# Memory peaks of batches 2 to 7 by VectorE and GpSimd instead of TensorE, with another plan of the order

## The chip, the cores and the metric

The kernel runs on one core of one Trainium2 chip. The metric is device time in microseconds (us) of one execution; runs of one kernel are compared by their medians. The engines are named as the profile names them: PE is TensorE (PEld its weight loads), DVE is VectorE, ACT is ScalarE, POOL is GpSimd, SP is SyncE, which issues nearly all DMAs.

## The reference, cut to what matters

Attention over 32 learned memories per head feeds a mixture of experts of which each token uses one. There are 8 batches, 8 heads, 576 tokens, 64 columns per head.

```python
a = phi - np.max(phi, axis=2, keepdims=True)        # softmax over the 576 tokens, for each memory
a = np.exp(a)
a = a / (np.sum(a, axis=2, keepdims=True) + 1e-09)
k_m = np.einsum('bhsm,bhsd->bhmd', a, k)            # 32 memory keys and values per head
v_m = np.einsum('bhsm,bhsd->bhmd', a, v)
scores = scale * np.matmul(q, k_m.transpose(0, 1, 3, 2))
attn = softmax(scores)                               # over the 32 memories
x = np.matmul(attn, v_m)                             # (tokens, 8 * 64), heads side by side
...
e_idx = np.argmax(x @ w_gate + modality_bias[modality_id], axis=1)
h = np.maximum(x[mask] @ w1[e], 0.0)                 # expert e of the token, 512 -> 1024 -> 512
out[mask] = gate_w[mask, None] * (h @ w2[e])
```

The change concerns the first line: the maximum of `phi` over the tokens, for each head and memory, and how it comes back to all rows before the subtraction.

## The kernel before, in words

**The work of one batch.** It has two halves that are woven together. The *attention* half: `mem_max` (maxima of `phi`), `mem_top`, `mem_exp` (subtract and exponential), `mem_sums`, `mem_kv` (memory keys and values), `mem_turn` (their transposes), `scores`, then the softmax in small steps (`soften`, `normalise`, `a_split`), `mem_gate`, `logits` and `gate`. The *expert* half: `value_weights` (memory values times the expert's first matrix, L645), `hidden` (L678: 8 column blocks of 6 matmuls for each of two parts of the tokens, then relu `hh` on ACT, L687, and rest `hl` on DVE, L690) and `outputs` (L707: tiles of 24 matmuls of 512 columns, then `ob` on ACT, L720, and the store). A float is carried as two halves, high and low, so each product takes three matmuls.

**The layout of `phi`.** One tile `ph` holds a batch: the 128 partitions are 2 groups of heads (g) by 64 rows of tokens, the free axis is 4 heads (j) by 9 tokens by 32 memories. `mem_max` folds the 9 tokens on DVE with four tensor_tensor (L259, L260, L262, L263; 512, 256, 128 and 128 columns) into `top`, 128 x (4 heads x 32 memories). What is left is a maximum over the 64 partitions of each group. Before, `mem_top` turns `top` on PE (L143) and reduces on DVE over the 64 columns of each group (L274, `topc`); `mem_exp` spreads the result again over 64 partitions with two PE matmuls against the identity (L288), and the subtraction (L294) reads it from PSUM. Then ACT takes the exponential (L297) and GpSimd folds the sums over tokens (`mem_sums`, L259 to L263 on POOL). `kv_products` has 72 small products (L328, of two passes each) and 8 for the sums (L336), which wait for GpSimd. `kv_divide` makes a reciprocal on DVE (L412, L414) and scaled copies `keys` and `values` on ACT (L424, L422); `mem_turn` turns them on PE (L143) and copies them out on ACT (`kT`, L454, `vT`, L462); `scores` (L504) needs `kT`.

**What sets the order.** Every engine works its instructions in the order in which the program issues them. `weave` issues the stages of the two halves: each half has a fixed list; the attention's stages have a due time in units of expert progress. `TAKES` gives each stage kind an estimated PE time and a chain of other engines' times ("D1.9" is 1.9 us of DVE, A is ACT, P is POOL), with which `weave` keeps a clock, the time when each engine is free, and when a stage may go. An expert stage that starts a product takes one of four PSUM banks in a ring (`ps_e`, `bufs=4`): block f + 4 of `hidden` may start once `hl` of block f is done. The experts' list has `value_weights` of the next batch within the third and the fourth tile of `outputs` (for batch 1: right behind the third and within the fourth); it needs `mem_turn` of that batch, and the experts go no further until it is issued.

## Time and profile before

| | |
|---|---|
| median of 3 runs | 402.3 us (402.03 to 402.81) |
| the profiled execution | 401.36 us |
| its span, first to last instruction | 399.6 us |
| granted TensorE clock | 0.993 |
| busy, share of the span | PE 96%, PEld 77%, DVE 60%, ACT 36%, POOL 10% |
| DMA | 56.91 MB, mean 142 GB/s |

How to read it: rows of the timeline and of the chain of work that ended last begin with the start in us from the span's start and the duration in us; a row's `xN` merges N instructions. Matmuls are pipelined, so a matmul's record is longer than its share of PE: what it costs is read from start to start. The group rows give `busy us, mean ns` behind the bar, then the idle time before the group.

### The profile page before, as it was taken

Reading aid. Unit: us, or ns where it says so; the run is one execution under the profiler, and the core shown is the slowest. Engines: PE = TensorE matmul, PEld = TensorE weight load, DVE = VectorE, ACT = ScalarE, POOL = GpSimd, SP = SyncE. Lnnn points to the kernel's source line nnn. Section 1 sums busy time; section 2 is a strip of 40 time slices with the busy share of each in tenths; the row PEclk is TensorE's granted clock in tenths of the full one; section 3 lists DMA queues with packets and bytes.
Section 4 is the critical chain, followed back from the end, with each engine's and each line's share of the span. In section 5 each row is a group of like instructions: output and inputs, shape, how many; then the busy total and the mean of one; then the engine's idle time right before and its main releaser. Section 6 shows DMA issues by size and latency. Waiting matters only on the chain.

```text
span 399.6 us, 10090 instructions
## 1 busy us (share of the span) xinstructions
PE 385.6 (96%) x4235; PEld 306.5 (77%) x4235; DVE 239.1 (60%) x588; ACT 143.6 (36%) x342; POOL 40.7 (10%) x87
## 2 busy tenths in 40 slices
PE   6889999999999999999999999999999999999993
PEld 2547885979779787787878878788867879687982
DVE  2687857875697366744686546863488437770400
ACT  1255333516243333432443323433442425340410
POOL 4158020002000200020000200002000200000000
PEclk9999999999999999999999999999999999999999
DMA  6999158525740671627411391614411011341112
GB/s 229 356 381 389 41 157 315 201 107 138 281 131 28 209 260 55 224 72 269 143 26 54 89 345 38 244 47 132 160 26 30 26 30 29 132 159 28 30 27 59
DMA packets 28967, 56.91 MB, mean 142 GB/s; under 512 B 3312, under 2 KB 8432, under 8 KB 28912
## 3 DMA queue, kind: packets, MB, share of 16 engines
q1 hardware_dynamic: 28624, 56.16, 42.1%
q8 instruction: 35, 0.57, 0.6%
q14 instruction: 20, 0.16, 0.1%
q10 hardware_dynamic: 288, 0.01, 0.0%
HBM read 37.29 MB, written 18.87 MB: 141 GB/s over the span
## 4 chain that ended last, share of the span: by engine, by line
PE 90%; DVE 5%; DMA 1%; ACT 1%; issue 1%; ACTq 0%
PE pe L707 52%; PE pe L678 23%; PE pair L328 4%; PE pe L645 4%; PE pair L504 3%; DMA ph<-in_phi_dram 1%; PE pair L592 1%; PE pair L143 1%; PE pair L162 1%; PE pair L288 1%; DVE vwl L658 1%; PE pair L353 1%; DVE hl L690 1%; DVE t2top L259 0%; DVE q_sb L492 0%
## 5 line engine op out<-in xcount | busy, mean ns | idle before, releaser
L707 PE MATMUL pe<-w2h,hh 128*128 128x512 f32 x288 | 117.9, 410 | 0.4 <-DVE hl L690 0.4
L707 PE MATMUL pe<-w2h,hl 128*128 128x512 f32 x288 | 112.4, 390 | 0.0
L707 PE MATMUL pe<-w2l,hh 128*128 128x512 f32 x288 | 110.5, 392 | 0.0
L690 DVE SCALAR_TENSOR_TENSOR hl<-pe,hh 128x256 fp32r<-128x256 f32 (+2 forms) x160 | 58.8, 394 | 50.9 <-ACT hh L687 50.2
L707 PEld LDWEIGHTS pe<-w2h,hh 128*128 128x128 f32 x288 | 54.0, 188 | 23.9 <-issue 11.5
L687 ACT ACTIVATE hh<-pe 128x256 fp32r<-128x256 f32 (+2 forms) x160 | 53.8, 362 | 37.9 <-PE pe L678 36.7
L707 PEld LDWEIGHTS pe<-w2l,hh 128*128 128x128 f32 x288 | 54.0, 188 | 12.1
L707 PEld LDWEIGHTS pe<-w2h,hl 128*128 128x128 f32 x288 | 54.2, 188 | 9.5
L720 ACT ACTIVATE ob<-pe,gates 128x512 f32<-128x512 f32 x36 | 24.7, 689 | 80.7 <-PE pe L707 39.9
L678 PE MATMUL pe<-xbh,vwh 128*128 128x320 f32 x128 | 39.7, 310 | 0.0
L678 PE MATMUL pe<-xbl,vwh 128*128 128x320 f32 x128 | 39.4, 308 | 0.0
L678 PE MATMUL pe<-xbh,vwl 128*128 128x320 f32 x128 | 39.4, 307 | 0.0
L678 PE MATMUL pe<-xah,vwh 128*128 128x256 f32 x128 | 36.0, 290 | 0.2 <-DVE hl L690 0.2
L259 POOL TENSOR_TENSOR t2sums<-exp 128x512 f32<-128x512 f32 x7 | 9.0, 1288 | 259.0 <-ACT exp L297 259.0
L678 PE MATMUL pe<-xal,vwh 128*128 128x256 f32 x128 | 35.1, 283 | 0.0
L678 PE MATMUL pe<-xah,vwl 128*128 128x256 f32 x128 | 35.0, 282 | 0.0
L531 DVE STREAM_TRANSPOSE a<-pair 128x256 f32<-128x256 f32 (+1 forms) x32 | 13.6, 461 | 24.3 <-PE pair L504 24.3
L678 PEld LDWEIGHTS pe<-xah,vwh 128*128 128x128 f32 x128 | 23.9, 191 | 1.9 <-DVE hl L690 1.0
L678 PEld LDWEIGHTS pe<-xbh,vwh 128*128 128x128 f32 x128 | 24.0, 187 | 0.6 <-issue 0.3
L678 PEld LDWEIGHTS pe<-xal,vwh 128*128 128x128 f32 x128 | 24.0, 191 | 0.3
L678 PEld LDWEIGHTS pe<-xbl,vwh 128*128 128x128 f32 x128 | 24.0, 188 | 0.3
L678 PEld LDWEIGHTS pe<-xbh,vwl 128*128 128x128 f32 x128 | 24.0, 188 | 0.0
(135 smaller groups left out, 436.1 us busy)
## 6 DMA issues: line engine op xcount, KB each, us to landing
kv_sb<-in_k_dram SPq DMA_DIRECT2D x8, 1152.0 KB, 5.5
kv_sb<-in_v_dram SPq DMA_DIRECT2D x8, 1152.0 KB, 9.5
out_dram<-ob SPq DMA_DIRECT2D x64, 128.0 KB, 2.4
q_sb<-in_q_dram SPq DMA_DIRECT2D x7, 1152.0 KB, 6.8
ph<-in_phi_dram SPq DMA_DIRECT2D x8, 576.0 KB, 4.2
raw<-in_moe_w_dram SPq DMA_DIRECT2D x2, 1024.0 KB, 9.8
raw<-in_moe_w_dram SPq DMA_DIRECT2D x1, 1280.0 KB, 11.3
out_dram<-ob SPq DMA_DIRECT2D x4, 256.0 KB, 2.1
```

The source lines that it names most:

```text
L143: nc.tensor.transpose(dst, src, ident[:rows, :rows])
L162: nc.tensor.matmul(idle, lhsT=busy[:, 0:P], rhs=busy, start=True, stop=True)
L259: eng.tensor_tensor(t2, src[:, :, 0:4 * M], src[:, :, 4 * M:8 * M], op=op)
L328: nc.tensor.matmul(live["kvp"][M * j:M * (j + 1), g], lhsT=pe[half, j, c * M:(c + 1) * M], rhs=kv_sb[half, :, j, c * D:(c + 1) * D], start ...
L504: nc.tensor.matmul(sc[g][M * j:M * (j + 1), a, c0 * BL:(c0 + n) * BL].rearrange("p (c t) -> p c t", t=BL), lhsT=kTs[b % 2][p0:p0 + BL, u, ...
L531: nc.vector.transpose(a[:, g].rearrange("p a c m -> p a (c m)"), sc[g][:, :, RA * part * BL:(RA * part + n) * BL])
L645: nc.tensor.matmul(pvs[g][M * j:M * (j + 1), :], lhsT=vT[b][rows, j, :], rhs=raw1[rows, j, cols], start=True, stop=True, tile_position=(D ...
L678: nc.tensor.matmul(ph[:, 0:n], lhsT=(vl if k == 2 else vh)[:, g, cols], rhs=xl if k == 1 else xh, start=(g == k == 0), stop=(g == NG - 1 a ...
L687: nc.scalar.activation(hs[0][:, f, h0:h0 + p1 - p0], ph[:, p0:p1], AF.Relu)
L690: nc.vector.scalar_tensor_tensor(hl, ph[:, p0:p1], 0.0, hh.bitcast(F32), op0=ALU.max, op1=ALU.subtract)
L707: nc.tensor.matmul(po, lhsT=tile_columns(hl if n == 1 else hh, f, t), rhs=(w2l if n == 2 else w2h)[:, f, :], start=(f == n == 0), stop=(f ...
L720: nc.scalar.activation(ob, po, AF.Copy, scale=gate_of(b, t))
```

## The change

For batches 2 to 7, `mem_top` is replaced by three stages. `mem_turn_top`: a DVE transpose of `top` in blocks of 32 x 32, after which the 32 rows of a block lie along the free axis, and a reduce over them (`tm`, 128 x 4). `mem_swap`: four GpSimd copies of 32 partitions x 4 columns that exchange neighbouring blocks of 32 partitions (`ts`), since a group's 64 partitions are two such blocks. `mem_peak`: DVE takes the larger of `tm` and `ts`, spreads it along 32 columns and transposes back (`peaks`). `mem_exp` then reads `peaks` from SBUF. Batches 0 and 1 keep the PE way. The PE transpose and the PE spreading of six batches are gone.

The plan changes with it. A time with T is DVE work that the plan keeps apart from GpSimd's: it starts no earlier than GpSimd is free, and a P time no earlier than the last T has ended. The sums cost GpSimd 2.9 instead of 0.5, and `kv` may start 1.8 before they are done. DVE work may run ahead of the clock by a margin that depends on the next expert stage and on how long the work is, instead of 1.0 or 3.5 alike. A count of PE instructions in pieces of 256 keeps `kv` from starting in the last 96 of a piece. Batches start earlier (`AHEAD`), the query transposes of batch 1 are due earlier.

```diff
+    def mem_turn_top(b):
+        top = live.pop(("top", b)).rearrange("p j m -> p (j m)")
+        tt = wk.tile([P, HG, BL], F32, name="tt")
+        nc.vector.transpose(tt.rearrange("p j t -> p (j t)"), top)
+        tm = wk.tile([P, HG], F32, name="tm")
+        nc.vector.tensor_reduce(tm, tt, axis=AX.X, op=ALU.max)
...
+    def mem_swap(b):
+        ts_ = wk.tile([P, HG], F32, name="ts")
+        for a in range(HG):
+            o = a ^ 1
+            nc.gpsimd.tensor_copy(ts_[BL * a:BL * (a + 1)], live["tm"][BL * o:BL * (o + 1)])
...
+    def mem_peak(b):
+        tm = live["tm"]
+        nc.vector.tensor_tensor(tm, tm, live["ts"], op=ALU.max)
+        tb = wk.tile([P, HG, BL], F32, name="tt")
+        nc.vector.tensor_copy(tb, tm.rearrange("p (j o) -> p j o", o=1).broadcast_to([P, HG, BL]))
+        peak = wk.tile([P, HG, BL], F32, name="peaks")
+        nc.vector.transpose(peak.rearrange("p j m -> p (j m)"), tb.rearrange("p j t -> p (j t)"))
...
     def mem_exp(b):
...
+        if b > 1:
+            peak = live["peak", b].rearrange("p j (o m) -> p j o m", o=1)
+        else:
+            topc = live["topc", b]
+            pb = bank("mem")
...
     TAKES = {
-        "max": (0.0, "D1.9"), "guess": (0.0, "D0.4"), "top": (0.3, "D0.25"),
+        "max": (0.0, "T1.9"), "guess": (0.0, "D0.4"), "top0": (0.3, "D0.25"), "ttop": (0.0, "D0.5"), "swap": (0.0, "P0.8"), "top": (0.0, "T0.6"),
...
-    AHEAD, SPREAD = (5.0, 4.0), 0.55
+    AHEAD, SPREAD = (5.8, 5.0), 0.55
...
-    plan_turns(1, 11.0, 0.9, floor=36.7)
+    plan_turns(1, 10.0, 0.9, floor=36.7)
...
-        HOLD = (1.0, 3.5)
+        PIECE, SHORT = 256, {"kv": 320, "k0": 320, "v0": 288, ...}
+        count = 350
+        HOLD = {"h0": 1.9, "h1": 2.4, "h3": 2.2}
...
-            t = max([0.0] + [done[n] + 0.1 for n in s[0][2] if n[0] != "g"])
+            t = max([0.0] + [done[n] + (0.1 if n[0] != "sums" else -1.8) for n in s[0][2] if n[0] != "g"])
...
+            if s[0][1] == "kv" and count % PIECE > PIECE - 96:
+                t = FAR
...
-                ra = max(ra, free["D"] - HOLD[not ex or ex[0][0][0] != "h"])
+                work = sum(float(x[1:]) for x in TAKES[at[0][1]][1].split() if x[0] in "DT")
+                ra = max(ra, free["D"] - (HOLD[ex[0][1]] - work if ex and ex[0][1] in HOLD else 3.5))
...
-                t = free[x[0]] = max(t, free[x[0]]) + float(x[1:])
+                eng = "D" if x[0] == "T" else x[0]
+                t = max(t, free[eng], free["P"] if x[0] == "T" else locked if x[0] == "P" else 0.0) + float(x[1:])
+                free[eng] = t
+                if x[0] == "T":
+                    locked = t
```

Three places show what moves; in the changed kernel the line numbers are 30 higher from `mem_exp` on (L690 is L720 there, L294 is L324).

DVE in batch 4, before, from `mem_max` to the reciprocal of `kv`; `hl` are the rests of `hidden`:

```order
L690 SCALAR_TENSOR_TENSOR hl<-pe,hh 128x256 x2
L259 TENSOR_TENSOR t2top<-ph_103 128x512
L260 TENSOR_TENSOR t2top<-t2top 128x4x64
L262 TENSOR_TENSOR top<-t2top 128x128
L263 TENSOR_TENSOR top<-top,ph_103 128x128
L690 SCALAR_TENSOR_TENSOR hl<-pe,hh 128x256 x6
L274 TENSOR_REDUCE topc<-pair_2402 128x2
L294 TENSOR_TENSOR exp<-ph_103,pair_2414 128x4x160
L294 TENSOR_TENSOR exp<-ph_103,pair_2414 128x4x128
L412 TENSOR_SCALAR den<-pair_2443 128x2
```

The same place now:

```order
L263 TENSOR_TENSOR top<-top,ph_103 128x128
L720 SCALAR_TENSOR_TENSOR hl<-pe,hh 128x256 x4
L284 STREAM_TRANSPOSE tt<-top 128x128
L286 TENSOR_REDUCE tm<-tt 128x4
L720 SCALAR_TENSOR_TENSOR hl<-pe,hh 128x256 x2
L300 TENSOR_TENSOR tm<-tm,ts 128x4
L302 COPY tt<-tm 128x128
L304 STREAM_TRANSPOSE peaks<-tt 128x128
L720 SCALAR_TENSOR_TENSOR hl<-pe,hh 128x256 x2
L324 TENSOR_TENSOR exp<-ph_103,peaks 128x4x160
L324 TENSOR_TENSOR exp<-ph_103,peaks 128x4x128
```

`mem_max` has moved ahead of all eight `hl` of `hidden`'s first part, and the new DVE work stands in two pieces between them, with GpSimd's swap running under two `hl`.

DVE in batch 6, now, where all of it stands behind the eight `hl`:

```order
L720 SCALAR_TENSOR_TENSOR hl<-pe,hh 128x256 x8
L259 TENSOR_TENSOR t2top<-ph_103 128x512
L260 TENSOR_TENSOR t2top<-t2top 128x4x64
L262 TENSOR_TENSOR top<-t2top 128x128
L263 TENSOR_TENSOR top<-top,ph_103 128x128
L284 STREAM_TRANSPOSE tt<-top 128x128
L286 TENSOR_REDUCE tm<-tt 128x4
L300 TENSOR_TENSOR tm<-tm,ts 128x4
L302 COPY tt<-tm 128x128
L304 STREAM_TRANSPOSE peaks<-tt 128x128
L324 TENSOR_TENSOR exp<-ph_103,peaks 128x4x160
```

Before, `mem_max` of this batch stood between the fourth and the fifth `hl`; now the swap has no `hl` to run under, and PE has 36 matmuls of `outputs` before `kv`, where it had 24.

ACT behind `kv` of batch 1, before:

```order
L424 ACTIVATE keys<-pair_929,rec 128x2x64 x2
L422 ACTIVATE values<-pair_929,rec 128x64 x2
L454 COPY kT_79<-pair_1036 128x256
L462 COPY vT_81<-pair_1036 128x128
L720 ACTIVATE ob<-pe,gates 128x512
```

And now:

```order
L454 ACTIVATE keys<-pair_937,rec 128x2x64 x2
L452 ACTIVATE values<-pair_937,rec 128x64 x2
L750 ACTIVATE ob<-pe,gates 128x512
L484 COPY kT_79<-pair_1043 128x256
L492 COPY vT_81<-pair_1043 128x128
```

On PE, `kv` of batch 1 comes six matmuls of `outputs` later than before. Between `kv` and the transposes stood nine of them and now six; between the transposes and `scores` stood three and now none. So `ob` of that tile gets ahead of the copy `kT`.

## The prediction

> **What bounds the kernel now.** I read the page first: the span, the busy shares, the chain of work that ended last.

> ```profile
> span 399.6 us, 10090 instructions
> PE 385.6 (96%) x4235; PEld 306.5 (77%) x4235; DVE 239.1 (60%) x588; ACT 143.6 (36%) x342; POOL 40.7 (10%) x87
> PE 90%; DVE 5%; DMA 1%; ACT 1%; issue 1%; ACTq 0%
> ```

> PE is the bound: it is busy 96% of the span and carries 90% of the chain. So time is won in two ways only, by PE work that goes away and by PE waits that go away, and lost by new PE waits. DVE at 60% matters where PE or ACT waits for it. The first difference in PE's order comes near 40 us, so the start is not touched.

> **The PE work removed.** The timeline of PE around the transpose of one batch and around the spreading of another:

> ```profile
> 87.03 0.39 PE L707 MATMUL pe<-w2h,hl 128*128 128x512 f32 x1
> 87.25 0.40 PE L707 MATMUL pe<-w2l,hh 128*128 128x512 f32 x1
> 87.48 0.28 PE L143 MATMUL pair<-ident,top 128*128 128x128 f32 x1
> 87.52 0.48 PE L707 MATMUL pe<-w2h,hh 128*128 128x512 f32 x1
> 87.83 0.39 PE L707 MATMUL pe<-w2h,hl 128*128 128x512 f32 x1
> ...
> 173.96 0.40 PE L707 MATMUL pe<-w2l,hh 128*128 128x512 f32 x1
> 174.29 0.44 PE L288 MATMUL pair<-ident,topc 128*64 128x128 f32 x4
> 175.00 0.39 PE L707 MATMUL pe<-w2h,hl 128*128 128x512 f32 x1
> ```

> Matmuls start 0.22 to 0.23 apart (87.03 to 87.25). From 87.25 to 87.83 there are two such steps, 0.45, and it took 0.58: the transpose costs 0.13. From 173.96 to 175.00 there are again two, and it took 1.04: the spreading costs 0.59. I take 0.70 a batch and 6 batches: **-4.2**. PE is back to back here, so all of it lies on the path. Of the 0.59, a part is the break itself: the step ahead of the block is 0.33 instead of 0.23, and entering again costs about as much, 0.2 for a break. In the new order PE's 512- and 256-to-320-column runs are entered 47 times instead of 61; 12 of the 14 are the removed pieces, two more are small blocks that now stand together: **-0.4**.

> **PE waits that go.** The chain and PE's timeline where `hidden` meets DVE work:

> ```profile
> 168.65 0.42 DVE hl L690
> 170.49 0.29 DVE top L263
> 170.78 0.34 DVE hl L690
> ...
> 170.61 0.28 PE L678 MATMUL pe<-xal,vwh 128*128 128x256 f32 x1
> 170.73 0.28 PE L678 MATMUL pe<-xah,vwl 128*128 128x256 f32 x1
> 171.17 0.39 PE L678 MATMUL pe<-xah,vwh 128*128 128x256 f32 x1 [0.16 <-DVE hl L690]
> ...
> 220.68 1.26 ACT exp L297 x2
> 222.19 0.28 PE L678 MATMUL pe<-xah,vwl 128*128 128x256 f32 x1
> 222.72 0.50 PE L707 MATMUL pe<-w2h,hh 128*128 128x512 f32 x1 [0.24 <-DVE hl L690]
> 265.49 0.28 PE L678 MATMUL pe<-xah,vwl 128*128 128x256 f32 x1
> 265.94 0.50 PE L707 MATMUL pe<-w2h,hh 128*128 128x512 f32 x1 [0.16 <-DVE hl L690]
> ```

> The step is 0.12 here (170.61 to 170.73), and 0.44, 0.53 and 0.45 at the three places: 0.32 + 0.41 + 0.33 = 1.06. The first and the third have `mem_max` between two `hl` (168.65 + 0.42 to 170.78: 1.71 us), the second the exponentials ahead of two `hh`. A check: six matmuls of 0.12 make a block of 0.72; with four banks `hl` may come 3 x 0.72 = 2.16 after its block ends, and needs about 0.85 for `hh` and itself, so DVE has 1.3 to spare, and 1.71 - 1.3 = 0.4 is about what PE lost. In the new order `mem_max` of batch 4 comes ahead of all `hl` and that of batch 6 behind them, and the exponentials of batch 5 behind its eighth `hl`: **-1.05**. The second kind is `kv` that waits for GpSimd's sums:

> ```profile
> 57.79 2.18 PE pair L328 x144
> 60.23 2.27 PE pe L707 x9
> 98.79 2.08 PE pair L328 x138
> 101.01 2.27 PE pe L707 x9
> 132.19 2.18 PE pair L328 x144
> 134.63 2.27 PE pe L707 x9
> ...
> 56.74 1.29 POOL L259 TENSOR_TENSOR t2sums<-exp 128x512 f32<-128x512 f32 x1 [17.76 <-ACT exp L297]
> 59.45 0.46 POOL L263 TENSOR_TENSOR sums<-sums,exp 128x128 f32<-128x128 f32 x1
> ```

> From `kv`'s start to the next run it is 2.22 at 98.79 and 2.44 at 57.79 and 132.19, where the sums (56.74 to 59.91, 3.17 us) end late: 0.22 twice, **-0.45**; in the new order both `kv` start later.

> **PE waits that come.** Batch 1, ACT's timeline behind `kv`:

> ```profile
> 60.79 0.63 ACT L424 ACTIVATE keys<-pair,rec 128x128 f32<-128x128 f32 x2 [3.88 <-DVE rec L414]
> 62.87 0.37 ACT L454 COPY kT<-pair 128x256 f32<-128x256 f32 x1 [1.04 <-PE pair L143]
> 63.62 0.69 ACT L720 ACTIVATE ob<-pe,gates 128x512 f32<-128x512 f32 x1 [0.21 <-ACT vT L462]
> ```

> Count from 60.23, where `outputs` goes on. Keys and values take ACT until about 1.6. With six matmuls (1.5) PE is at the transposes about when they are ready, so up to 0.2 is lost there; then `ob` (0.69) holds ACT until 2.3 and `kT` (0.37) until 2.7, while PE, with nothing between, could begin `scores` at about 1.8. The experts cannot fill in: their next stage needs this very transpose. Behind `scores` stand all of PE's work and the softmax of batch 1. I take **+1.0** (0.7 if `ob` slips behind, 1.3 with the wait for the second copy). In the later batches at least 3 matmuls of `outputs` and a block of `hidden` stand between, 1.4 us, which covers `ob` and `kT`.

> **The new DVE and GpSimd work.** None of it is in the trace. The nearest rows:

> ```profile
> L597 DVE STREAM_TRANSPOSE lgT<-pair 128x160 f32<-128x160 f32 x8 | 2.8, 350 | 6.6 <-PE pair L592 6.6
> L228 POOL CAST mid_f<-mid 64x4 f32<-64x4 int32 x2 | 0.4, 184 | 0.0
> ```

> The two transposes, the reduce and the spreading copy are 128 columns or less: at most 0.35 each, I take 0.30, and 0.15 for the small maximum; 1.35 a batch, less the 0.29 that L274 took (the size of L263 above): 6.4 us more on an engine that is idle 40%. What it hides under is the 1.3 of slack: the pieces are 0.6 and 0.75, so no block of `hidden` waits. A swap copy I price at 0.18, the four-column row, with 0.08 between GpSimd's instructions (four of the fold take 3.17, of which 2.94 are work): 1.05 a swap. The ends: nothing, or 0.46, the 128-column row, 2.2 a swap. In batches 3 and 4 it runs under two `hl`, 1.44. What is queued behind the waiting maximum on DVE are the next `hl` and the exponentials, and behind those the sums and `kv`. Batch 6, from the start of the last matmul of `hidden`'s first part: `hl` done 1.1 (0.28, then `hh` and `hl` of 0.42), `mem_max` 1.7, turn and reduce 0.65, swap 1.1, peak 0.85, subtractions and exponentials 2.1, sums 3.3 with the hand-over: 10.8. PE comes to L336 after 36 matmuls (8.4) and 2.1 of `kv`: 10.5. **+0.3**. In batches 3 to 5 the same sum without the first four is 6.5, against 21 matmuls and `kv`, 7.0: covered with 0.5 to spare. Batches 2 and 7 have several us.

> SP: one load of `phi` goes out two stores earlier, needed a batch later; no load goes later: nothing. The margin of 96 instructions moves only `kv` of batch 7; the other new costs and margins act through the order alone.

> [...] The row first:

> ```profile
> 37.69 1.29 POOL L738 TENSOR_TENSOR w2l<-t2sums,w2h 128x512 fp32r<-128x512 f32 x1
> 37.87 1.79 DVE L537 TENSOR_TENSOR a<-a,mx 128x640 f32<-128x640 f32 x1
> L537 DVE TENSOR_TENSOR a<-a,mx 128x640 f32<-128x640 f32 x8 | 7.5, 942 | 0.1
> ```

> Seven of the eight average 0.82 (7.5 less 1.79, over 7); the one that began under a GpSimd instruction ended 0.68 after it (38.98 to 39.66), so it stood still. [...]

> **The sum.** -4.2 - 0.4 - 1.05 - 0.45 + 1.0 + 0.3 = -4.8. Made against the profiled execution, 401.36 (399.6 of span), that is 396.6; the execution lies 0.9 under the median, so on the median 402.3 - 4.8 = **397.5**.

> **The rivals.**
> *The swap is dear.* At 2.2 instead of 1.05 batch 6 loses 1.1 more, batches 3 to 5 0.6 each beyond their 0.5: +2.9, **400.4**. For it: no copy across partitions of this size is in the trace's busy part. Against: the four-column row.
> *Waits eat it all.* If what happens in batch 1 happens in five more, +4.8, **402.3**. For it: ACT has `ob` ahead of `kT` in some of them. Against: the 1.4 us of other PE work there. That the removed work was not on the path would end here too; the back-to-back starts speak against it.
> [...]
> *Slower: PE waits for code.*

> ```profile
> q8 instruction: 35, 0.57, 0.6%
> ```

> 35 packets share 0.6% of 16 engines' 399.6 us, 1.1 each. If the seven moved `kv`, PE's densest instructions, met such a packet in full: +7.7, **405.2**. Against: no `kv` above shows a gap beyond the sums' wait.

> **How the numbers follow.** Forecast 0.64, dear swap 0.16 (both faster), no change 0.09, held DVE 0.07, code 0.04 (both slower). A change of 0.2%, 0.8 us, is about what this measurement can tell: faster 0.80, same 0.09, slower 0.11. Low: neither new wait, 396.2, taken as 396.0. High: beyond the dear swap and halfway to no change, 401.3.

> **What would show it.** Right: no L143 with `top` and no spreading after 60 us; PE busy about 4 us less; no step beyond 0.35 in `hidden`; one wait near 63 us between the transposes and `scores`; GpSimd copies near 0.2. Wrong: copies of 0.4 or more, the maximum on DVE waiting long with `hl` behind it, L336 late in several batches, or steps inside `kv`.

## The result, and the profile after

| | before | changed |
|---|---|---|
| median | 402.16 us (401.50 to 402.81, 4 runs) | 397.52 us (397.34 to 397.81, 4 runs) |
| the profiled execution, its span | 401.36, 399.6 | 397.34, 395.6 |
| TensorE busy | 385.6 | 380.6 |
| VectorE, GpSimd busy | 239.1, 40.7 | 244.5, 45.3 |

The ratio is 0.9889, with a 95% interval from 0.9871 to 0.9908: 4.6 us less by the medians, 4.0 by the two profiled executions. The ratios here and below leave out two far longer executions on record, 627.93 us of one experiment and 1293.24 us of the kernel before. The page of the changed kernel, in the places shown of before, and the groups of the new work:

```profile
span 395.6 us, 10092 instructions
PE 380.6 (96%) x4205; PEld 305.6 (77%) x4205; DVE 244.5 (62%) x612; ACT 143.4 (36%) x342; POOL 45.3 (11%) x111
PE 90%; DVE 4%; ACT 2%; DMA 1%; POOL 1%; issue 1%; ACTq 0%; POOLq 0%
L294 POOL COPY ts<-tm 32x4 f32<-32x4 f32 x24 | 4.8, 199 | 202.3 <-DVE tm L286 201.5
L304 DVE STREAM_TRANSPOSE peaks<-tt 128x128 f32<-128x128 f32 x6 | 1.9, 312 | 0.2
L284 DVE STREAM_TRANSPOSE tt<-top 128x128 f32<-128x128 f32 x6 | 1.8, 308 | 0.1
L286 DVE TENSOR_REDUCE tm<-tt 128x4 f32<-128x128 f32 x6 | 1.7, 287 | 0.2
L302 DVE COPY tt<-tm 128x128 f32<-128x128 f32 x6 | 1.4, 228 | 0.2
L300 DVE TENSOR_TENSOR tm<-tm,ts 128x4 f32<-128x4 f32 x6 | 0.9, 158 | 1.2 <-POOL ts L294 1.0
```

PE is still the bound and has 5.0 us less to do. The new DVE instructions are 7.7 us, less six L274 of 0.29; the idle time ahead of L300, 1.2 in all, is the only time that DVE stood for the swap, and 1.0 of it is one batch.

The waits of PE that are new (the columns: us in total, times, longest), and the chain around the first, in batch 1:

```profile
PE pair L534 <- ACT kT L484: 0.7, 1, 0.7
PE pair L366 <- POOL sums L263: 0.3, 1, 0.3
```

```profile
61.33 1.26 PE pe L737 x5
62.59 0.42 ACT values L452 x2
63.00 0.32 issue
63.33 0.69 ACT ob L750
64.01 0.27 ACT kT L484
...
64.33 1.74 PE pair L534 x58
```

`ob` goes ahead of `kT` on ACT, and `scores` starts at 64.33. Read from start to start, PE loses 0.28 ahead of the transposes and 0.90 between them and `scores`: 1.18. The second is in batch 6, on the chain from the maximum to the sums:

```profile
263.55 0.42 DVE hl L720
...
266.06 0.30 DVE tm L286
...
266.48 0.18 POOL ts L294
...
267.14 0.19 POOL ts L294
267.36 0.17 DVE tm L300
...
267.81 0.32 DVE peaks L304
268.16 0.83 DVE exp L324
...
273.19 0.46 POOL sums L263
...
273.69 0.27 PE pair L366 x13
```

From the end of the reduce (266.36) to the small maximum (267.36) the swap takes 1.00. From start to start PE loses 0.55 at L366. The three waits for `hl` that stood before are not among the waits of the changed kernel, and no step inside `hidden` loses more than 0.18.

### The profile page after: what moved, and what is told of

The parts are those of the page before. It is cut to its first block, busy times and chain, and to the rows that moved or that the text cites. A ratio compares the mean times of both kernels' runs of the same rounds, so it can differ in the third digit from the quotient of the medians.

```text
span 395.6 us, 10092 instructions
## 1 busy us (share of the span) xinstructions
PE 380.6 (96%) x4205; PEld 305.6 (77%) x4205; DVE 244.5 (62%) x612; ACT 143.4 (36%) x342; POOL 45.3 (11%) x111
## 4 chain that ended last, share of the span: by engine, by line
PE 90%; DVE 4%; ACT 2%; DMA 1%; POOL 1%; issue 1%; ACTq 0%; POOLq 0%
PE pe L737 49%; PE pe L708 26%; PE pe L675 4%; PE pair L534 3%; PE pair L358 3%; DMA ph<-in_phi_dram 1%; PE pair L622 1%; PE pair L162 1%; PE pair L143 1%; DVE vwl L688 1%; PE pair L383 1%; PE pair L675 0%; PE pair L511 0%; ACT ob L750 0%; DVE t2top L259 0%
## 5 line engine op out<-in xcount | busy, mean ns | idle before, releaser
L737 PE MATMUL pe<-w2h,hh 128*128 128x512 f32 x288 | 116.4, 404 | 0.0
L720 DVE SCALAR_TENSOR_TENSOR hl<-pe,hh 128x256 fp32r<-128x256 f32 (+2 forms) x160 | 59.1, 393 | 54.2 <-ACT hh L717 53.3
L294 POOL COPY ts<-tm 32x4 f32<-32x4 f32 x24 | 4.8, 199 | 202.3 <-DVE tm L286 201.5
L148 ACT CAST vwh<-pe 128x512 fp32r<-128x512 f32 x28 | 15.0, 588 | 25.8 <-PE pe L675 25.8
```

Source lines behind the costliest of these rows:

```text
L148: nc.scalar.copy(h, src)
L294: nc.gpsimd.tensor_copy(ts_[BL * a:BL * (a + 1)], live["tm"][BL * o:BL * (o + 1)])
L720: nc.vector.scalar_tensor_tensor(hl, ph[:, p0:p1], 0.0, hh.bitcast(F32), op0=ALU.max, op1=ALU.subtract)
L737: nc.tensor.matmul(po, lhsT=tile_columns(hl if n == 1 else hh, f, t), rhs=(w2l if n == 2 else w2h)[:, f, :], start=(f == n == 0), stop=(f ...
```

## The experiments

The two halves of the change are told apart first: the new order with the old peaks, and the new peaks in the old order.

**The new order alone.** `kernel` as changed, with the peaks of all batches by TensorE:

```diff
-        if b > 1:
+        if b > B:
...
-        peaks = ((("top0", [("max", b)], mem_top, 1.5),) if b < 2 else (
+        peaks = ((("top0", [("max", b)], mem_top, 1.5),) if b < B else (
```

> The changed plan (its times, margins and early starts), but batches 2 to 7 get their peaks by TensorE as before. Theory A (PE is the bound, and the gain is PE work taken out): the six transposes and spreadings come back at 0.70 a batch, 4.2 us, and two breaks, 0.4; the wait of 0.55 for the sums in batch 6 may go, since the chain to the exponentials is shorter again: 401 to 402 us. Rival B (the new order made the gain, by the waits that it removed): it stays near 397.5, at most 399.

Measured: 405.03 us, ratio to before 1.0073 (1.0046 to 1.0100). Neither theory had that. The chain shows one place:

```profile
94.62 2.08 PE pair L358 x138
96.71 0.10 PE pair L366 x10
96.80 2.33 issue
99.14 0.23 PE pair L366 x3
```

PE stands 2.33 us within the last products of batch 2's `kv`, and nothing that the profile shows is waited for. Of the trace's 35 instruction packets of 16 KB one starts at 96.79, lasts 0.95, and PE goes on 1.4 after its end. Counted in the trace (matmuls, weight loads and PE's semaphore events), this `kv` begins 136 instructions past a multiple of 256. That made code the suspect; the next two runs move the code and nothing else.

**The new order alone, its code 32 instructions earlier.**

```diff
-    BUSY = 86, 10
+    BUSY = 70, 10
```

> The kernel with the new order and the old peaks on TensorE in all batches, with 16 fewer of the small matmuls ahead of the first batch (70 instead of 86), so that every later TensorE instruction stands 32 places earlier: batch 2's kv products then begin 104 past a multiple of 256 instead of 136, a place from which the changed kernel's batch 7 (103) ran without a gap. Theory A (the 2.33 us gap was late code): it is gone and the time is 405.0 - 2.4 = 402.6 us (402.2 to 403.0), which is the time of the kernel before. Rival (the gap belongs to the new order itself): 405.0 us (404.6 to 405.4).

Measured: 402.25 us, ratio 0.9991 (0.9973 to 1.0009). The gap within `kv` is gone. The chain at the same place:

```profile
95.19 2.08 PE pair L358 x138
97.27 0.13 PE pair L366 x14
97.40 1.97 PE pe L708 x12
99.37 0.23 issue
```

What is left of it is a stand of 0.23 in `hidden` behind `kv`; there too PE goes on 1.38 after the end of a 16 KB packet (98.22). So the gap belongs to the place of the code, and the new order by itself is worth nothing that this measurement can tell: with the TensorE peaks it gains the `hl` waits and pays batch 1's.

**The changed kernel, its code 96 instructions later.**

```diff
-    BUSY = 86, 10
+    BUSY = 134, 10
```

> The changed kernel with 48 more of the small matmuls that keep TensorE busy ahead of the first batch (134 instead of 86); all later work is the same and in the same order, but every one of its TensorE instructions stands 96 places later in the program. In the run of the new order with the old peaks TensorE stood 2.33 us without a wait inside batch 2's kv products, just as a 16 KB instruction packet began, and its kv products began 136 instructions past a multiple of 256 as the trace counts them; in the changed kernel none of the seven does between 104 and 174. Theory A (the gap is code that arrives late, and it depends on where a kv block begins among the pieces of 256): with the shift batches 5 (140) and 6 (133) get such a gap, 3 (159) and 4 (122) perhaps, 2.3 us each: 402 us with two, 399.8 to 404.5 in all. Rival (the gap came of something else, a transfer or a wait that the trace doesn't show): no gap follows the shift, 397.5 us (397.2 to 398).

Measured: 402.75 us, ratio 1.0000 (0.9982 to 1.0018). The whole gain is lost by a shift of code. The gaps are in batches 5 and 6, the two named, whose `kv` begin 140 and 133 past a multiple of 256. (This trace lacks three matmul records, 4250 beside 4253 weight loads; counted by the loads, the places are those of the expectation.) Batch 3 (159) has none; in batch 4 (122) PE stands 0.33 shortly behind `kv`. The chain in the three:

```profile
180.00 0.33 issue
...
227.74 0.08 PE pair L366 x8
227.82 1.27 issue
...
276.06 1.80 issue
...
278.08 2.99 PE pe L737 x9
```

The packets here end at 178.96, 227.68 and 276.47, and PE goes on 1.38, 1.41 and 1.39 after. These stands make 3.4 of the 5.5 us by which this span is longer. Another part follows the last: nine matmuls that take 2.28 elsewhere take 2.99. Two windows of that stretch, cut where the granted clock changes (PE's busy time is the first behind the window's length; the columns behind the busy times: granted clock, DMA share, GB/s):

```profile
275.98:279.39 3.41, 1.61 (x22) 1.29 (x9) 1.23 (x4) 0.81 (x4) 0.00 (x0) 1.00 0.79 233
279.39:282.80 3.41, 3.41 (x12) 2.62 (x11) 1.74 (x3) 0.76 (x4) 0.00 (x0) 0.50 1.05 405
```

Batch 6 stands for its sums (0.57 from start to start) and then at the end of `kv` (1.80), and 1.5 us after that the granted clock is 0.50 for 3.41 us, which costs up to 1.7 (half of the 3.41, an estimate). With the stands that is 5.1 of the 5.5 us; the rest I have not assigned.

**The new peaks in the old order.** The planner's rules and numbers of the kernel before, the three new stages in place of `mem_top`:

```diff
-    AHEAD, SPREAD = (5.8, 5.0), 0.55
+    AHEAD, SPREAD = (5.0, 4.0), 0.55
...
-        HOLD = {"h0": 1.9, "h1": 2.4, "h3": 2.2}
+        HOLD = (1.0, 3.5)
...
-            if s[0][1] == "kv" and count % PIECE > PIECE - 96:
-                t = FAR
```

> The plan of before (its times, margins, starts), but batches 2 to 7 get their peaks on VectorE and GpSimd. Theory A says PE work of 4.6 us goes, but the old plan reckons 0.5 us for the sums' GpSimd time and lets the exponentials of batch 2 stand behind all sixteen rests of the hidden layer, so that kv finds 7.5 us of chain (peaks 0.75, exponentials 2.1, sums 3.3, hand-overs) and only 4.9 us of PE work ahead of its last products: 2.6 us lost there and 0.5 to 1.5 in three or four other batches; with the four waits of before kept, 401 to 405 us. Rival C (the peaks alone carry the gain, the plan is ballast): 397 to 399 us.

Measured: 406.75 us, ratio 1.0113 (1.0082 to 1.0143), over the first theory's range. PE's waits and the windows around the first of them, in batch 2:

```profile
PE pair L366 <- POOL sums L263: 2.5, 3, 1.6
PE pair L143 <- ACT values L452: 1.6, 1, 1.6
```

```profile
102.51:105.92 3.41, 1.25 (x88) 0.89 (x70) 0.46 (x3) 0.04 (x1) 2.25 (x4) 1.00 0.79 226
105.92:109.34 3.42, 1.74 (x11) 0.72 (x19) 2.52 (x4) 1.53 (x6) 0.00 (x0) 0.50 1.03 400
109.34:112.75 3.41, 3.41 (x80) 1.11 (x64) 1.29 (x2) 1.07 (x2) 0.00 (x0) 0.50 0.61 234
```

In the old order the swap, the second transpose and the sums come too late for `kv`: PE stands 1.0 ahead of it, 1.8 for the sums and 1.8 for the scaled copies behind, and runs at half clock from 105.92 to 112.75, 6.8 us. The forecast had 2.6 lost in this batch and no word of the clock. The 4.2 us of PE work saved are in this kernel as well (PE busy is 383.8 with those slow matmuls in it), and the waits take more. So each half alone gives nothing or a loss, and together they give 1.1%: the order's worth is that it makes room for the peaks' longer chain. From the new order without the gap (0.9991) to the whole change (0.9889) it is 1.0%, 4.1 us, for the peaks.

**The swap three times as long.** Twelve copies a batch instead of four, to the same places with the same values:

```diff
-        for a in range(HG):
+        for a in 3 * list(range(HG)):
```

> The changed kernel with every swap copy on GpSimd made three times (12 copies a batch instead of 4, to the same places with the same values; nothing else is moved). In the changed kernel's trace the copies start every 0.22 us, so the swap grows by 8 x 0.22 = 1.76 us in each of six batches. Theory A (the swap lies on the way from the maximum to the kv products, with little to spare): batch 6, where TensorE already waits for the sums, takes the whole 1.76, batches 3 and 4 become waits of about 1 us each, the others lose little: 401.5 to 403.5 us. Rival (the swap lies beside other work and has slack everywhere but in batch 6): 397.5 to 399.3 us, with one wait of at most 2.3 us ahead of a sums matmul.

Measured: 404.87 us, ratio 1.0048 (1.0026 to 1.0070): slower than before the change, and over the first theory's range.

```profile
PE pair L366 <- POOL sums L263: 4.3, 3, 1.6
PE pair L358 <- ACT exp L327: 0.6, 1, 0.6
```

Batches 3, 4 and 6 wait, as the first theory named. Start to start it is 1.61, 1.61 and 0.76 + 1.80, where the changed kernel has 0.55 in batch 6 alone: 5.2 more, and 0.44 in batch 2. Batches 3 and 4 had 0.3 to spare and not the 0.7 that the expectation took (0.235 a copy makes 1.9, of which 1.6 shows).

**The swap on VectorE.**

```diff
-            nc.gpsimd.tensor_copy(ts_[BL * a:BL * (a + 1)], live["tm"][BL * o:BL * (o + 1)])
+            nc.vector.tensor_copy(ts_[BL * a:BL * (a + 1)], live["tm"][BL * o:BL * (o + 1)])
```

> The changed kernel with the four swap copies on VectorE instead of GpSimd; the order of the steps is the same. Theory A (what the chain pays for the swap on GpSimd is the two hand-overs, about 0.15 us each, and 0.02 of pitch for each copy; VectorE has room): batch 6's wait for the sums shrinks from 0.55 to between 0 and 0.3, 397.2 us (396.8 to 397.6). Rival (VectorE is close to the bound in the batch's first part, so that 0.8 us more on it make the splits of hidden late): waits of TensorE for hl come back, 398 to 399.5 us.

Measured: 398.78 us beside 402.83 for before, ratio 0.9896 (0.9873 to 0.9919). The interval holds that of the changed kernel nearly whole, so the time tells nothing. In the trace PE's loss at L366 in batch 6 is 0.27 instead of 0.55, which is the first theory's size, no wait for `hl` comes back, and the span is 395.2 beside 395.6. Half of batch 6's wait is thus the way over GpSimd:

```profile
266.73 0.69 DVE L294 COPY ts<-tm 32x4 f32<-32x4 f32 x4
```

From the end of the reduce to the small maximum it is 0.75 here instead of 1.00. Most of the 0.25 is the copies, which follow each other closer (0.69 instead of 0.84); the rest is the two hand-overs, where the expectation had it the other way round.

**The two waits taken away.** First the margin by which DVE work may run ahead of `hidden`'s second kind of block, which puts `kv` of batch 1 six matmuls earlier:

```diff
-        HOLD = {"h0": 1.9, "h1": 2.4, "h3": 2.2}
+        HOLD = {"h0": 1.9, "h1": 2.9, "h3": 2.2}
```

> The changed kernel with one number changed, the margin of DVE work ahead of h1 blocks, 2.4 to 2.9. Batch 1's exponentials then stand between the sixth and the seventh rest, kv of batch 1 has the place that it had before, and kT is copied ahead of ob. Theory A: the steps of 0.28 and 0.90 that PE lost around 63 us are gone, 396.3 us, 0.3% under the changed kernel. Rival D (PE's waits are made up for later, because a late PE finds banks and buffers free that it would have waited for): no difference, 397.5.

Measured: 396.85 us, ratio 0.9858 (0.9833 to 0.9883). The chain in batch 1:

```profile
61.21 2.30 PE pe L737 x9
63.51 0.33 PE pair L143 x3
63.84 0.70 PE pe L737 x3
64.54 1.53 PE pair L534 x63
```

Nine matmuls stand ahead of the transposes again and three behind them, and nothing waits. Then that and batches 2 to 7 started 0.4 earlier:

```diff
-    AHEAD, SPREAD = (5.8, 5.0), 0.55
+    AHEAD, SPREAD = (5.8, 5.4), 0.55
```

> As the run with the margin of 2.9, and batches 3 to 7 start a little earlier (AHEAD 5.4 instead of 5.0), so that batch 6 has its maxima and swap ahead of or between the rests of the hidden layer as batches 3 to 5 have. Theory A: the 0.55 that kv of batch 6 waited for the sums goes as well: 395.8 us, 0.45% under the changed kernel. Rival D: 397.5, or a new wait elsewhere that eats it.

Measured: 396.52 us, ratio 0.9860 (0.9830 to 0.9890). The wait for the sums in batch 6 is gone from the trace too, but the time is over the first theory's 395.8. The intervals of both touch that of the changed kernel (0.9871 to 0.9908): the waits are gone for sure, their price by the time alone is not.

**The new peaks from the second batch on.** On top of both numbers:

```diff
-        if b > 1:
+        if b > 0:
...
-        HOLD = {"h0": 1.9, "h1": 2.9, "h3": 2.2}
+        HOLD = {"h0": 1.9, "h1": 3.3, "h3": 2.2}
```

> The kernel with both planner's numbers raised (HOLD h1, AHEAD) and the new peaks from the second batch on instead of the third, with h1 at 3.3 so that the wait ahead of batch 1's scores does not come back. Theory A (each batch whose peaks leave TensorE is worth 0.70 us as long as no wait takes their place): 396.0 us (395.6 to 396.3) beside 396.5 with both numbers alone, and no wait of TensorE over 0.35 between 55 and 75 us. Rival (in batch 1 the sums come later by the swap and the second transpose, and the products wait for them, or VectorE's longer first part delays the keys): a wait of 0.5 to 1.5 us between 55 and 75 us, 396.5 to 397.5.

Measured: 396.29 us, ratio 0.9843 (0.9817 to 0.9870), span 393.4. This is the best of all kernels here; its interval ends where that of the changed kernel begins. No wait came back in batch 1:

```profile
59.48 2.30 PE pe L737 x9
...
62.80 1.53 PE pair L534 x63
```

**Without the margin of 96.** The rule that holds `kv` back is left out:

```diff
-            if s[0][1] == "kv" and count % PIECE > PIECE - 96:
-                t = FAR
```

> The changed kernel without the planner's rule that keeps the kv products away from the last 96 places of a piece of 256 instructions; only batch 7's kv products move, 78 TensorE instructions earlier by the planner's count (to 188 of 256 by it). By the trace's count they begin about 25 past a multiple of 256 instead of 103, and the runs so far had gaps only where they begin between 127 and 136. Theory A (the planner's count runs away from the chip's: 2886 where the trace has 2223, 8202 where it has 7271, so that the rule guards the wrong places): no gap, 397.5 us (397.1 to 398.0), as with the rule. Rival (the rule is right): a gap of 1.4 to 2.3 us in batch 7's kv products, 399 to 400 us.

Measured: 398.13 us, ratio 0.9896 (0.9867 to 0.9925), no gap in any `kv`. The rule gains nothing here, since its count is not the program's: for batch 2's `kv` in the run with the first gap it had 30 past a multiple of 256, a place that it allows, and the trace has 136.

## Why the prediction was right, point by point

Mechanism and size were right. That the forecast of 397.5 met the median to 0.02 us is luck: between the two profiled executions, for which the sum was made, it is 4.0 us and not 4.8, the two new waits came out 0.43 longer together than forecast, and the interval of the ratio is 0.75 us to either side.

**Work removed, -4.2.** Right: no L143 with `top` and no spreading after 60 us, PE busy 5.0 less (about 4 was named), and 1.0%, 4.1 us, between the two kernels that differ in the peaks alone. Here the removed work was all on the path, as the back-to-back starts said. The -0.4 for two more breaks is within what the runs cannot tell apart.

**Waits that go, -1.05 and -0.45.** The `hl` waits are gone. But the new order with TensorE's peaks, where they are gone too and batch 1's wait has come, is 0.09% under before with an interval of 0.18% to either side: this agrees with -1.05 - 0.45 - 0.4 + 1.2 = -0.7 us (0.17%), and the time shows no single term. The trace of the changed kernel shows the second: from `kv`'s start to the next run it is 2.22 in batch 1 (59.11 to 61.33) and 2.21 in batch 3, where it was 2.44.

**Batch 1, +1.0.** Measured 1.18: 0.28 ahead of the transposes (up to 0.2 was allowed) and 0.90 for `kT`, which is the 2.7 - 1.8 of the working. The cause is as told, since nine and three matmuls around the transposes take it away.

**Batch 6, +0.3.** Measured 0.55. Both sides of the sum were off by a little, in the same direction. From the last matmul of `hidden`'s first part, at 262.75, the chain to the sums took 10.94 (273.69), not 10.8; PE would have been there after 10.4 (273.69 - 0.55), not 10.5. Within the chain the swap is 1.00 (1.1 taken) and the peak 0.77 (0.85). Too short were the first step, 1.22 until `hl` is done (1.1 taken, without the hand-overs between matmul, `hh` and `hl`), and the subtractions and exponentials, 2.22 (2.1). In batches 3 and 4 the sum left 0.5 to spare; the longer swap found 0.3.

**The new costs.** A copy takes 0.18, with 0.22 from one to the next; 0.18 was taken from the four-column row, so the dear swap fell. That rival is real at its price. No run shows the held DVE, which had a chance of 0.07: at 2.9 us a swap (twelve copies, from 271.02 to 273.96 in batch 6) the kernel is slower than before, ratio 1.0048, but it was the sums that came late, 4.3 us of waits at L366, and not the `hl`. DVE rose by 5.4, 6.4 was forecast.

**GpSimd beside VectorE.** In batch 2 the swap begins while a subtraction of 0.81 runs on VectorE. The timeline of the changed kernel, that subtraction and then the swaps of batches 2 and 3:

```profile
87.10 0.81 DVE L605 TENSOR_TENSOR xbl<-aT,xbh 128x640 fp32r<-128x640 f32 x1
87.31 1.30 POOL L294 COPY ts<-tm 32x4 f32<-32x4 f32 x4 [26.48 <-DVE tm L286]
...
127.73 0.84 POOL L294 COPY ts<-tm 32x4 f32<-32x4 f32 x4 [31.97 <-DVE tm L286]
```

1.30 instead of 0.84: the first copy took 0.64, from 87.31 to 87.95, and the subtraction ended at 87.91. The other five swaps took 0.84. So the first copy ended 0.04 after the subtraction; why it took longer beside it is not shown. It cost nothing there, since that batch has several us to spare: its sums were done at 95.77, and PE came to them at 99.39.

**PE waits for code.** The forecast held against this rival, and the changed kernel has no such gap. But the reason given, that no `kv` before showed one, was weak: a shift of 96 instructions brings two, with a third stand behind a `kv`, and loses the whole gain, and the new order alone has one. The changed kernel is clear of it by where its code happens to lie, not by its rule. 0.04 was too small a chance for that.

## What to carry to other kernels

Work taken off the bounding engine pays in full only if the longer chain on the other engines has its room in the order: here the peaks without the plan lose 1.1%, the plan without the peaks gains nothing, and both gain 1.1%. When a kernel that issues the same work gets slower, look for waits that the profile calls "issue" inside dense runs of small matmuls, and shift the code by a few dozen instructions before the order is blamed: here 32 took a stand of 2.33 us away, and 96 brought stands of 1.27 and 1.80. And in a chain of short steps count what lies between the instructions as well: four swap copies of 0.18 take 1.00 from the reduce to the maximum.

## What the runs showed of the hardware that was not expected

**Half clock after a long stand.** The granted clock is 0.50 from 279.39 to 282.80 in the shifted kernel, which is 3.41 us, and from 105.92 to 112.75, 6.83 and so twice that, with the peaks in the old order. The windows just ahead, shown above, have PE busy for 1.61 and 1.25 of 3.41 us. Two other runs have long stands as well, the new order alone its gap of 2.33 and the triple swap 0.76 and 1.80 in batch 6. Their windows, carried on in steps of 3.41 from the changes of their own clocks (that such steps go on through the full clock is an assumption of mine):

```profile
95.08:98.49 3.41, 1.72 (x137) 1.64 (x124) 0.56 (x2) 0.14 (x2) 0.92 (x2) 1.00 0.57 153
277.88:281.29 3.41, 1.86 (x81) 1.45 (x68) 0.61 (x3) 0.19 (x1) 2.10 (x4) 1.00 0.42 87
```

After these the clock stayed at 1.00. (In the old order the window from 105.92, busy for 1.74 but at half clock, was followed by another at 0.50.) So it isn't the length of the stands in all that tells the cases apart, 2.37 in the shifted kernel and 2.56 in the triple swap, but, by my estimate, how much of them falls into one window; that the limit lies between 1.61 and 1.72 of busy time is read from these four alone, and what sets the clock is not shown.
